# Transposes of K and Q by VectorE from 32x32 blocks loaded in place, instead of by TensorE, in a DeltaNet and feed-forward kernel

## The chip, the cores and the metric

The kernel runs on one core of one Trainium2 chip. The metric is the time on the device of one execution, in microseconds (us), as the median of several. The mean clock of TensorE over the whole span varied between 0.92 and 0.98 from run to run of the kernel before with no matching change of time; I read clocks only by stretch and never alone. In the views PE is TensorE's matmuls and PEld its weight loads; DVE is VectorE, ACT ScalarE, POOL GpSimd, SP SyncE, and a q after the name is the engine's DMA queue. The granted clock is the share of its full clock that TensorE was given (1.00 is all of it).

## The reference

Four batches, eight heads, 768 tokens, head size 48, all fp32. Attention is a delta rule, a recurrence over tokens; a layer norm and a two-layer feed-forward follow.

```python
for t in range(S):
    kt, vt, bt = k_n[:, :, t], v[:, :, t], beta[:, :, t, None]     # k_n: keys of length 1
    y[:, :, t] = einsum('bhd,bhde->bhe', q[:, :, t], state)
    v_old = einsum('bhde,bhd->bhe', state, kt)
    state = state + bt[..., None] * einsum('bhd,bhe->bhde', kt, vt - v_old)
# x = y with its heads side by side, (4, 768, 384); xn = layer norm of x times g_ln
out = x + maximum(xn @ w_ch1, 0) @ w_ch2                           # 384 -> 1536 -> 384
```

## The kernel before

The kernel works in 12 chunks of 64 tokens. Within a chunk the recurrence becomes a triangular system. `prep` forms K^T, Q^T and the products K·K^T (the "grams") and K·Q^T; `blocks` sends the grams through DRAM and inverts 32x32 blocks on VectorE in a long loop of short instructions; `join` combines the blocks by small matmuls (p_e, p_z); `recur` applies the state (p_by, p_u, p_s, p_by again); `ffn` is the feed-forward, the big matmuls p_h and p_o. The weights arrive as 64-bit floats and are converted on VectorE (w_sb). Everything is emitted by a plan with a time for each step, and the build lays out the order of instructions of each engine. Only the first part, up to the first joins, is held to the order of emission.

What the change touches:

```python
def load(dst, src, c, engs):                       # rows of 48 numbers into 64-wide slots
    for e in range(2):
        engs[e % len(engs)].dma_start(out=dst[e*C:(e+1)*C, :, 0:D], in_=src[...])
def load_all(c):                                   # 6 loads a chunk, all in SyncE's queue
    load(kpads[c % NKP], k, c, (nc.sync,)); load(qpads[c % NQP], q, c, (nc.sync,))
    load(vs[c], v, c, (nc.sync,))

def turned(c, g, n):                               # 4 TensorE transposes, 1 eviction by ScalarE
    p_t = ps_att([128, NP, 128], "p_t")
    for j in range(NP):
        nc.tensor.transpose(p_t[:, j], src[:, g*H+2*j : g*H+2*j+2], ident)
    nc.scalar.copy(made[c][0][g][:, :, n], p_t)

# in recur: 48 columns of keys a matmul, then two updates of the state
nc.tensor.matmul(p_s[DP*hp : DP*hp+D, ...], kp[half(e), 2*j+hp, 0:D], u[...])
for hp in range(2):
    nc.vector.tensor_tensor(out=new, in0=new, in1=p_s[DP*hp : DP*hp+D, ...], op=ALU.add)
# (cut)
first_join(0); first_join(1)                       # one after the other
```

## Time and profile before

| | before |
|---|---|
| median of 3 (range) | 675.39 us (674.75 to 676.48) |
| span of the profiled run | 673.2 us |
| start to the first weight converted after the joins | 86.2 us |
| from there to the end of the last conversion | 76.2 us |
| from there to the end ("late") | 510.8 us, TensorE busy 95% |

### The profile page before, as it was taken

The page shows a single profiled execution, that of the slowest core. Times are in us where ns is not written, and L with a number is a line of the kernel's source. Part 1 is how long each engine was busy: PE and PEld are TensorE (multiplying, and loading weights), DVE is VectorE, ACT ScalarE, POOL GpSimd, SP SyncE. Part 2 cuts the span into 40 slices and gives each one's busy share as a digit, 9 for nine tenths or more (in the row PEclk, how much of TensorE's full clock was granted, in tenths as well). Part 3 has the DMA queues.
Part 4 walks back from the last instruction along what each step waited for, and adds up shares of the span by engine and source line. Part 5 has one row for each costly group of instructions (what it writes and reads, how often), then busy time and mean ns, then how long its engine had stood idle before and what let it go on. Part 6 is the DMA issues. An engine that isn't in the chain of part 4 may idle for free.

```text
span 673.2 us, 18698 instructions
## 1 busy us (share of the span) xinstructions
PE 585.4 (87%) x8296; PEld 424.2 (63%) x8296; DVE 341.0 (51%) x870; ACT 180.5 (27%) x458; POOL 47.4 (7%) x78
## 2 busy tenths in 40 slices
PE   4214688968998989799899999899999899999997
PEld 4213576634865756686666786666876657768684
DVE  4542698999534695223964226944229742121100
ACT  3111343201332312241223432215421222213120
POOL 5000221111000101000100100101000000000000
PEclk9955577986999898599999999999999999999999
DMA  7975066851423415222305332023211020010000
GB/s 173 185 101 83 4 159 161 194 134 38 108 56 52 66 25 110 56 60 41 60 32 92 85 72 59 13 66 60 60 49 25 32 46 14 1 25 2 16 8 24
DMA packets 135824, 44.58 MB, mean 66 GB/s; under 512 B 128832, under 2 KB 131904, under 8 KB 135744
## 3 DMA queue, kind: packets, MB, share of 16 engines
q1 hardware_dynamic: 127392, 33.29, 25.5%
q0 software_dynamic: 1920, 9.44, 4.9%
q10 hardware_dynamic: 6432, 0.66, 0.8%
q8 instruction: 65, 1.06, 0.7%
q14 instruction: 15, 0.12, 0.1%
HBM read 29.48 MB, written 13.89 MB: 64 GB/s over the span
## 4 chain that ended last, share of the span: by engine, by line
PE 59%; DVE 26%; DMA 6%; issue 3%; SPq 3%; ACT 2%; DVEq 0%; ACTq 0%
PE p_o L631 20%; PE p_h L620 20%; DVE tmp L435 6%; DVE xb L440 6%; PE p_g L296 4%; PE p_t L285 3%; DMA kpad<-in_k_dram 2%; SPq L138 2%; PE p_e L465 2%; PE p_by L542 2%; PE p_z L506 2%; PE p_u L558 2%; DVE s L575 1%; PE p_s L569 1%; DVE full L259 1%
## 5 line engine op out<-in xcount | busy, mean ns | idle before, releaser
L631 PE MATMUL p_o<-w_sb,h_f 128*128 128x384 f32 x576 | 212.9, 507 | 9.2 <-DVE w_sb L263 9.2
L620 PE MATMUL p_h<-xnt,w_sb 128*128 128x256 f32 x864 | 210.5, 392 | 5.3 <-ACT h_f L625 5.1
L620 PEld LDWEIGHTS p_h<-xnt,w_sb 128*128 128x128 f32 x864 | 160.7, 193 | 32.5 <-ACT h_f L625 7.3
L631 PEld LDWEIGHTS p_o<-w_sb,h_f 128*128 128x128 f32 x576 | 104.2, 192 | 71.1 <-DVE w_sb L263 14.9
L625 ACT ACTIVATE h_f<-p_h 128x256 f32<-128x256 f32 x144 | 54.7, 383 | 129.1 <-PE p_h L620 128.7
L435 DVE TENSOR_TENSOR tmp<-xb,gb 128x31 f32<-128x31 f32 (+20 forms) x170 | 59.7, 351 | 4.2
L440 DVE TENSOR_TENSOR xb<-xb,tmp 128x31 f32<-128x31 f32 (+20 forms) x170 | 57.4, 338 | 4.4
L296 PE MATMUL p_g<-kqt 48*64 48x128 f32 (+1 forms) x896 | 33.3, 300 | 15.8 <-DVE pt L305 13.3
L296 PEld LDWEIGHTS p_g<-kqt 48*64 48x64 f32 x896 | 26.7, 163 | 24.0 <-DVE pt L305 12.6
L286 ACT COPY kqt<-p_t 128x512 f32<-128x512 f32 x48 | 27.9, 586 | 45.4 <-DVE w_sb L263 23.6
L638 DVE TENSOR_TENSOR o<-p_o,x_ln 128x384 f32<-128x384 f32 x24 | 13.3, 556 | 47.7 <-PE p_o L631 47.4
L575 DVE TENSOR_TENSOR s<-s,p_s 48x384 f32<-48x384 f32 x44 | 24.3, 552 | 25.9 <-PE p_s L569 25.3
L547 DVE TENSOR_TENSOR rhs<-v_raw,p_by 128x384 f32<-128x384 f32 x22 | 12.1, 552 | 45.6 <-PE p_by L542 45.6
L511 DVE COPY xt<-p_z 32x256 f32<-32x256 f32 x48 | 20.0, 416 | 27.7 <-PE p_z L506 27.1
L305 DVE TENSOR_TENSOR pt<-p_g,pmask 128x512 f32<-128x512 f32 x24 | 16.5, 688 | 34.1 <-ACT gsb L301 32.8
L525 DVE COPY u<-p_u 64x192 f32<-64x192 f32 x24 | 8.6, 359 | 47.7 <-ACT u L524 47.5
L542 PEld LDWEIGHTS p_by<-s,kqt 48*64 48x64 f32 x1408 | 23.2, 134 | 10.8 <-issue 8.9
L285 PE MATMUL p_t<-ident,qpad 128*128 128x128 f32 x96 | 17.7, 321 | 13.1 <-DMA qpad<-in_q_dram 12.5
L542 PE MATMUL p_by<-s,kqt 48*64 48x48 f32 x1408 | 26.4, 221 | 0.0
L465 PE MATMUL p_e<-xn,gsb 32*32 32x32 f32 x768 | 19.9, 207 | 7.3 <-DVE xn L457 7.0
L465 PEld LDWEIGHTS p_e<-xn,gsb 32*32 32x32 f32 x768 | 17.0, 121 | 13.2 <-issue 9.9
L285 PE MATMUL p_t<-ident,kpad 128*128 128x128 f32 x96 | 18.1, 323 | 7.8 <-POOL pmask L218 5.9
(78 smaller groups left out, 493.1 us busy)
## 6 DMA issues: line engine op xcount, KB each, us to landing
words<-in_moe_w_ch_dram POOLq DMA_DIRECT2D x24, 384.0 KB, 4.4
gd<-gsb SPq DMA_DIRECT2D x12, 512.0 KB, 3.5
qpad<-in_q_dram SPq DMA_DIRECT2D x24, 192.0 KB, 4.4
v_raw<-in_v_dram SPq DMA_DIRECT2D x24, 192.0 KB, 4.8
out_dram<-o SPq DMA_DIRECT2D x48, 96.0 KB, 2.2
kpad<-in_k_dram SPq DMA_DIRECT2D x22, 192.0 KB, 4.2
gb<-gd SPq DMA_DIRECT2D x40, 64.0 KB, 3.4
xd<-xb SPq DMA_DIRECT2D x5, 512.0 KB, 4.5
```

The costliest lines, as they stand in the source:

```text
L285: nc.tensor.transpose(p_t[:, j], src[:, h : h + 2], ident)
L286: nc.scalar.copy(made[c][0][g][:, :, n], p_t)
L296: nc.tensor.matmul(p_g[toks, hp, j, n0:n1], kqt[rows, j, 0, toks], kqt[rows, j, n0:n1, toks])
L435: nc.vector.tensor_tensor(out=t, in0=xb[:, :, 0:n, j : j + 1].to_broadcast([128, nb, n, w]), in1=gb[:, :, j : j + 1, j + 1 : L].to_broadca ...
L440: nc.vector.tensor_tensor(out=rest, in0=rest, in1=t, op=ALU.subtract)
L465: nc.tensor.matmul(p_e[r1, h % H], gsb[r0, h, BK:C], xn[r0, h])
L511: nc.vector.tensor_copy(out=xt[r0, g * H : (g + 1) * H, BK:C], in_=p_z[r0])
L542: nc.tensor.matmul(p_by[half(e ^ (hp & n)), hp, n, j], kqt[rows, j, n, half(e)], s[rows, e, j], start=(n == 0 and j == 0), stop=(n == 0), ...
L575: nc.vector.tensor_tensor(out=new, in0=new, in1=p_s[DP * hp : DP * hp + D, :, 0 : NP * D].rearrange("p e (j d) -> p e j d", d=D), op=ALU.add,)
L620: nc.tensor.matmul(p_h, w1_sb[:, t, f * 128 : (f + 1) * 128], xnt[:, t], start=(t == 0), stop=(t == KC - 1),)
L625: nc.scalar.activation(h_f, p_h, ACTF.Relu)
L631: nc.tensor.matmul(p_o, hs[f][:, g * 128 : (g + 1) * 128], w2_sb[:, f], start=(f == 0), stop=(f == FT - 1),)
```

## The change

The intent is to take 192 transposes and 48 evictions off TensorE and ScalarE. VectorE can transpose 32x32 blocks from SBUF to SBUF. If the DMA writes each 32-token by 32-feature block where its transpose belongs, 24 instructions do the whole. The keys as rows are still needed for norms and state; they are loaded later, unpadded, and p_s takes 64 columns of them, so that one update serves the whole state. The two first joins are interleaved, and the norms of the second chunk come after them. Not shown in the cut below: the first weight words are fetched later, and from chunk 2 on the raw loads, norms and scaling of a chunk are a step of their own (`prep_v`).

```diff
+def load_blocks(src, c, n, engs):                  # 8 DMAs for K, 8 for Q
+    dst = tblocks[(2 * c + n) % NTB]
+    for u in range(2):
+        for hp in range(2):
+            for m in range(2):
+                w = min(32, D - 32 * m)
+                engs[m % len(engs)].dma_start(out=dst[p0:p0+32, :, u, 0:w], in_=...)
+def load_turned(c):
+    load_blocks(k, c, 0, (nc.sync,))
+    load_blocks(q, c, 1, (nc.sync,))
-def turned(c, g, n):  # 4 x nc.tensor.transpose, nc.scalar.copy
+def turned(c, n):
+    nc.vector.transpose(made[c][0][:, :, n]..., tblocks[(2 * c + n) % NTB])
 ...
-    kp[half(e), 2 * j + hp, 0:D]
+    kp[half(e), h0 * D : h0 * D + DP]
-for hp in range(2):
-    nc.vector.tensor_tensor(out=new, in0=new, in1=p_s[...], op=ALU.add)
+nc.vector.tensor_tensor(out=s, in0=s, in1=p_s[...], op=ALU.add)
 ...
 next(inv)                     # first gathers
-for c in two: load(qpads[c], q, c, (nc.sync,))
+for c in two: load_blocks(q, c, 1, (nc.sync,))
+for c in two: load_kv(c)
 next(inv)
-(Q transposes by TensorE)
+for c in two: turned(c, 1)    # before the inverse loop, on its engine
 ...
+first joins 0 and 1 interleaved; after them:
+scale_v(1, norms(1), nc.vector)
 ...
-plan.once(times[0] - 20, load_all, chunks[0])
-plan.once(times[0] + 13 - 0.5, load_all, chunks[1])
+for i, c in enumerate(chunks):
+    plan.once(times[0] - 20 + 32.5 * i, load_turned, c)
```

More of the change, by code (lines that the diff above doesn't have):

```diff
@@ L108 @@
     const = ctx.enter_context(tc.tile_pool(name="const", bufs=1))
-    loads = ctx.enter_context(tc.tile_pool(name="loads", bufs=4))
+    loads = ctx.enter_context(tc.tile_pool(name="loads", bufs=3))
     work = ctx.enter_context(tc.tile_pool(name="work", bufs=2))
@@ L128, in ps_ffn @@
         return psum.tile(shape, FP32, name=name, tag="ffn", bufs=2)
-    NKP, NQP, NXT = 4, 2, 4
-    kpads = [const.tile([128, GH, DP], FP32, name=f"kpad{i}") for i in range(NKP)]
-    qpads = [const.tile([128, GH, DP], FP32, name=f"qpad{i}") for i in range(NQP)]
+    NXT, NTB = 4, 4
+    tblocks = [const.tile([128, GH, 2, 32], FP32, name=f"tb{i}") for i in range(NTB)]
+    NK = 3
+    kraws = [const.tile([128, GH * D + DP - D], FP32, name=f"k{i}") for i in range(NK)]
     vs = {}
-    def load(dst, src, c, engs):
+    def load_blocks(src, c, n, engs):
+        dst = tblocks[(2 * c + n) % NTB]
+        for u in range(2):
+            toks = slice(c * C + 32 * u, c * C + 32 * u + 32)
+            for hp in range(2):
+                for m in range(2):
+                    w = min(32, D - 32 * m)
+                    p0 = DP * hp + 32 * m
+                    engs[m % len(engs)].dma_start(
+                        out=dst[p0 : p0 + 32, :, u, 0:w],
+                        in_=src[:, hp::2, toks, 32 * m : 32 * m + w].rearrange("b j t d -> t (b j) d"),
+                    )
@@ L137, in load, with k_of, load_kv @@
+    def load(dst, src, c):
         for e in range(2):
-            engs[e % len(engs)].dma_start(
-                out=dst[e * C : (e + 1) * C, :, 0:D],
+            nc.sync.dma_start(
+                out=dst[e * C : (e + 1) * C],
                 in_=src[2 * e : 2 * e + 2, :, c * C : (c + 1) * C, :].rearrange("g h p d -> p (g h) d"),
             )
-    def load_all(c):
+    def k_of(c):
+        return kraws[c % NK][:, 0 : GH * D].rearrange("p (h d) -> p h d", d=D)
+    def load_kv(c):
+        load(k_of(c), k, c)
@@ L144, in load_all @@
         vs[c] = loads.tile([128, GH, D], FP32, name="v_raw")
-        load(kpads[c % NKP], k, c, (nc.sync,))
-        load(qpads[c % NQP], q, c, (nc.sync,))
-        load(vs[c], v, c, (nc.sync,))
-    for t in kpads[0:2]:
-        nc.vector.memset(t[:, :, D:DP], 0.0)
+        load(vs[c], v, c)
+    def load_turned(c):
+        load_blocks(k, c, 0, (nc.sync,))
+        load_blocks(q, c, 1, (nc.sync,))
+    for i in (0, 2, 1, 3):
+        for hp in range(2):
+            p0 = DP * hp + 32
+            (nc.vector if i in (0, 2) else nc.gpsimd).memset(tblocks[i][p0 : p0 + 32, :, :, D - 32 : 32], 0.0)
@@ L151 @@
     for c in range(2):
-        load(kpads[c], k, c, (nc.sync, nc.scalar))
-    for t in (*qpads, *kpads[2:]):
-        nc.gpsimd.memset(t[:, :, D:DP], 0.0)
+        load_blocks(k, c, 0, (nc.sync, nc.scalar))
     w1_sb = const.tile([128, KC, DFF], FP32, name="w1_sb")
@@ L174, in fetch_words @@
             )
-    for _ in range(3):
-        fetch_words()
     beta_b = const.tile([128, NSL, BK], FP32, name="beta_b")
@@ L223 @@
     xts = [const.tile([128, GH, C], FP32, name=f"xt{i}") for i in range(NXT)]
+    for t in kraws:
+        nc.gpsimd.memset(t[:, GH * D :], 0.0)
     for t in xts:
@@ L228 @@
         nc.gpsimd.memset(t, 0.0)
+    for _ in range(3):
+        fetch_words()
     scale_w = const.tile([128, KC + 1], FP32, name="scale_w")
@@ L276 @@
     made, grams, deep_pools = {}, {}, []
-    N_PREP = 1 + 2 * 3
-    def turned(c, g, n):
-        src = (kpads[c % NKP], qpads[c % NQP])[n]
-        p_t = ps_att([128, NP, 128], "p_t")
-        for j in range(NP):
-            h = g * H + 2 * j
-            nc.tensor.transpose(p_t[:, j], src[:, h : h + 2], ident)
-        nc.scalar.copy(made[c][0][g][:, :, n], p_t)
+    N_PREP = 4
+    def turned(c, n):
+        nc.vector.transpose(
+            made[c][0][:, :, n].rearrange("p i (u t) -> p i u t", t=32), tblocks[(2 * c + n) % NTB]
+        )
     def products(c, g, n0, n1):
-        kqt = made[c][0][g]
+        kqt = made[c][0]
         p_g = ps_two([128, 2, NP, 2, C], "p_g")
@@ L295, in products @@
                 toks = slice(C * e, C * e + C)
-                nc.tensor.matmul(
-                    p_g[toks, hp, j, n0:n1], kqt[rows, j, 0, toks], kqt[rows, j, n0:n1, toks]
-                )
+                i = (2 * e + g) * NP + j
+                nc.tensor.matmul(p_g[toks, hp, j, n0:n1], kqt[rows, i, 0], kqt[rows, i, n0:n1])
         heads = slice(g * H, (g + 1) * H)
@@ L311, in norms @@
     def norms(c):
-        kp = kpads[c % NKP]
         ksum = work.tile([128, GH], FP32, name="ksum")
@@ L316, in norms @@
             ksq = work.tile([128, H, D], FP32, name="ksq", bufs=1)
-            nc.scalar.square(ksq, kp[:, heads, 0:D])
+            nc.scalar.square(ksq, k_of(c)[:, heads])
             nc.vector.tensor_reduce(out=ksum[:, heads], in_=ksq, axis=mybir.AxisListType.X, op=ALU.add)
@@ L333, in new_chunk @@
         pool = deep_pools[0] if c % 4 == 0 and deep_pools else work
-        made[c] = ([pool.tile([128, NP, 2, 128], FP32, name="kqt", bufs=2 if pool is not work else 6) for _ in range(2)], [])
+        made[c] = (pool.tile([128, GH, 2, C], FP32, name="kqt", bufs=1 if pool is not work else 3), [])
     def prep(c):
         new_chunk(c)
-        scale_v(c, norms(c), nc.gpsimd)
-        yield
+        for n in range(2):
+            turned(c, n)
+            yield
         for g in range(2):
-            for n in range(2):
-                turned(c, g, n)
-                yield
             products(c, g, 0, 2)
@@ L346, in prep, with prep_v @@
         nc.sync.dma_start(out=grams[c][1], in_=grams[c][0])
+    def prep_v(c):
+        load_kv(c)
+        yield
+        with tc.issue_after(after) if c < 4 else nullcontext():
+            scale_v(c, norms(c), nc.gpsimd)
+        yield
     def prep_g(c):
         new_chunk(c)
-        for g in range(2):
-            turned(c, g, 0)
-            yield
+        turned(c, 0)
         for g in range(2):
@@ L492, in first_join @@
         nc.scalar.mul(es, p_e, -1.0)
+        yield
         p_z = ps_att([128, GH, FB], "p_z")
@@ L500, in first_join @@
             copy(out=xt[rows, :, c0 + FB : c0 + BK], in_=p_z[rows])
+        yield
     def last_z(xt, g, es, p_z, h):
@@ L528, in recur @@
     def recur(c, g):
-        kqt, pt = made[c][0][g], made[c][1][g]
+        kqt, pt = made[c][0], made[c][1][g]
         heads = slice(g * H, (g + 1) * H)
-        kp, xt, vv = kpads[c % NKP][:, heads], xts[c % NXT][:, heads], vs[c][:, heads]
+        kp, xt, vv = kraws[c % NK], xts[c % NXT][:, heads], vs[c][:, heads]
         s = states[g]
@@ L542, in recur @@
                         nc.tensor.matmul(
-                            p_by[half(e ^ (hp & n)), hp, n, j], kqt[rows, j, n, half(e)], s[rows, e, j],
+                            p_by[half(e ^ (hp & n)), hp, n, j], kqt[rows, (2 * e + g) * NP + j, n], s[rows, e, j],
                             start=(n == 0 and j == 0), stop=(n == 0), skip_group_check=True,
@@ L568, in recur @@
                 for hp, e in TILES:
+                    h0 = g * H + 2 * j + hp
                     nc.tensor.matmul(
-                        p_s[DP * hp : DP * hp + D, e, j * D : (j + 1) * D],
-                        kp[half(e), 2 * j + hp, 0:D], u[half(e), 2 * j + hp],
-                    )
-            for hp in range(2):
-                new = s[DP * hp : DP * hp + D]
-                nc.vector.tensor_tensor(
-                    out=new, in0=new,
-                    in1=p_s[DP * hp : DP * hp + D, :, 0 : NP * D].rearrange("p e (j d) -> p e j d", d=D),
-                    op=ALU.add,
-                )
+                        p_s[half(hp), e, j * D : (j + 1) * D],
+                        kp[half(e), h0 * D : h0 * D + DP], u[half(e), 2 * j + hp],
+                    )
+            nc.vector.tensor_tensor(
+                out=s, in0=s, in1=p_s[:, :, 0 : NP * D].rearrange("p e (j d) -> p e j d", d=D), op=ALU.add
+            )
             yield
@@ L653 @@
         for c in two:
-            first.spread(prep_g(c), 4, 4 * c, 4 * c + 4)
-        first.spread(weights(0, 3), 3, 0, 8)
+            first.spread(prep_g(c), 2, 4 * c, 4 * c + 4)
+        first.spread(weights(0, 3), 3, 8, 16)
         first.run()
@@ L659 @@
         for c in two:
-            load(qpads[c], q, c, (nc.sync,))
+            load_blocks(q, c, 1, (nc.sync,))
         for c in two:
-            vs[c] = loads.tile([128, GH, D], FP32, name="v_raw")
-            load(vs[c], v, c, (nc.sync,))
+            load_kv(c)
         next(inv)
         for c in two:
-            for g in two:
-                turned(c, g, 1)
+            turned(c, 1)
         for _ in inv:
@@ L670 @@
         for c in (2, 3):
-            load_all(c)
+            load_turned(c)
         load_beta()
-        knrms = []
-        for c in two:
-            knrms.append(norms(c))
-            for g in two:
-                products(c, g, 1, 2)
-        for c in two:
-            first_join(c)
+        for g in two:
+            products(0, g, 1, 2)
+        scale_v(0, norms(0), nc.vector)
+        joins = [first_join(c) for c in two]
+        next(joins[0])
+        for g in two:
+            products(1, g, 1, 2)
+        next(joins[0])
+        next(joins[1])
         joined = join(two)
         next(joined)
-        scale_v(0, knrms[0], nc.vector)
+        next(joins[1])
         next(joined)
-        scale_v(1, knrms[1], nc.vector)
-        for _ in joined:
-            pass
+        next(joined)
+        next(joined)
+        next(joined)
+        scale_v(1, norms(1), nc.vector)
     after = last[mybir.EngineType.DVE]
@@ L702 @@
         t0, t1 = starts[c], ends[c]
+        if c > 1:
+            plan.spread(prep_v(c), 2, t0 - 72, t0 - 12)
         plan.once(t0, begin, c)
```

## The prediction

> **What bounds the kernel now.** I first read parts 1 and 2 of the page, to see which engine is full and when:
>
> ```profile
> PE 585.4 (87%) x8296; PEld 424.2 (63%) x8296; DVE 341.0 (51%) x870; ACT 180.5 (27%) x458; POOL 47.4 (7%) x78
> ...
> PE   4214688968998989799899999899999899999997
> ...
> DVE  4542698999534695223964226944229742121100
> ...
> DMA  7975066851423415222305332023211020010000
> ```
>
> TensorE (PE) is full over the span but not everywhere: one slice is 16.8 us, and in the first five PE is mostly idle. VectorE (DVE) is full in slices 6 to 10. So I cut the span at the first matmul of the feed-forward stage (82 us) and at the last weight conversion (161.8 us), and asked for the busy time in the three stretches. Columns: stretch, length, then PE, PEld, DVE, ACT, POOL busy (instructions), granted clock, DMA share, GB/s.
>
> ```profile
> 0.00:82.00 82.00, 31.95 (x1148) 27.65 (x1148) 37.13 (x90) 19.13 (x43) 16.59 (x35) 0.72 0.65 112
> 82.00:162.40 80.40, 65.19 (x786) 44.84 (x782) 76.41 (x200) 20.55 (x51) 12.25 (x21) 0.80 0.57 139
> 162.40:674.00 511.60, 488.23 (x6368) 351.67 (x6368) 227.47 (x581) 140.87 (x364) 18.52 (x22) 0.98 0.22 47
> ```
>
> Three limits. **Start** (0 to 82): no engine is half busy; a chain of loads, DRAM round trips and short instructions sets the time. **Middle** (82 to 162): DVE is busy 76.4 of 80.4 us (95%), above all converting weights. **Late** (162 to the end): PE is busy 488 of 511.6 us (95%), so what PE is spared there comes off the end.
>
> The removed work, from the groups by line:
>
> ```profile
> L286 ACT COPY kqt<-p_t 128x512 f32<-128x512 f32 x48 | 27.9, 586 | 45.4 <-DVE w_sb L263 23.6
> L285 PE MATMUL p_t<-ident,qpad 128*128 128x128 f32 x96 | 17.7, 321 | 13.1 <-DMA qpad<-in_q_dram 12.5
> L285 PE MATMUL p_t<-ident,kpad 128*128 128x128 f32 x96 | 18.1, 323 | 7.8 <-POOL pmask L218 5.9
> L575 DVE TENSOR_TENSOR s<-s,p_s 48x384 f32<-48x384 f32 x44 | 24.3, 552 | 25.9 <-PE p_s L569 25.3
> ```
>
> These are 192 PE transposes, 35.8 us of PE busy time, with 48 evictions by ScalarE. The last line is the state update that the change merges from two instructions into one.
>
> ```profile
> L485 DVE STREAM_TRANSPOSE xn<-xt 128x1024 f32<-128x1024 f32 x2 | 2.5, 1240 | 0.0
> ```
>
> This is the price of the replacement: the kernel already has a 32x32-block transpose of 128x1024 on DVE, the shape of the new ones, at 1240 ns.
>
> **What the Trainium skill says.** "VectorE: DVE Perf Modes", section The three transpose paths: TensorE's full transpose goes to PSUM, VectorE's to SBUF but only in 32x32 blocks. The trace agrees: each four PE transposes have an eviction of 586 ns, and the DVE instruction writes SBUF itself. [...]192 B rows took 15 ns (median) but 19.7 on average[...]; 128 B packets (the DRAM round trips) took 13.5 and 64 B ones 10.3. "TensorE: Matmul & The Clock Gate", section LDWEIGHTS: the load time follows the number of columns. The trace agrees: 64-column groups (p_u) cost PE 13.93 us for 640, 48-column ones (p_s) 10.35 us for 576, or 21.8 and 18.0 ns each.
>
> **The change, part by part.**
>
> *Late stretch, PE.* The same windows for p_t alone give 7.37 us in the start, 7.91 in the middle and 19.94 in the late stretch (120 transposes, 30 groups of four). Busy spans overlap their neighbours; from one start to the next a group of four holds PE for 0.44 to 0.60 us (360.48 to 361.06, 387.92 to 388.36), say 0.55. So 30 x 0.55 = 16.5 us. Against it, p_s now loads 64 columns, not 48: 576 x (21.8 - 18.0) ns = +2.2 us. On DVE two transposes per chunk cost 2.5 us and the merged updates save 4 - 2 = 2 per chunk, 1.1 us; with DVE at 227 of 511 us that lies beside PE. One update fewer between p_s and the next p_by and no ACT copies in front of p_g may take 1.5 us from PE's small waits. Late: -16.5 + 2.2 - 1.5 = **-16 us**.
>
> *Middle, DVE.* PE loses 7.9 us there, but it waits for weights at the end (p_o for w_sb, 9.2 us in the waits), so that becomes idle time. DVE gains the transposes of chunks 2 and 3, 4 x 1.24 = 5.0, and loses four state updates, 2.2. The order of instructions shows weights and inverse steps interleaved nearly as before. I put this at **+2 us**.
>
> *Start.* Before, the chain runs: keys landed 11.6, transposes and products, both grams sent to DRAM at 17.3, blocks gathered 25.2, inverse loop 27.64 to 36.26, scattered back 42.7, norms and masked products, first-join transpose at 52.03 and 61.27, 32-wide joins from 70.5.
> (a) Keys: each row becomes 128 B + 64 B, about 25 ns for 19.7, so 4096 rows over 16 engines take 6.4 us for 5.0; but the weight words (1.15 MB, 2.9 us at 393 GB/s) are issued later and no longer mixed in. Transposing is 1.24 us for two PE groups and two copies. Grams about **-1 us**.
> (b) The order of instructions on DVE puts both Q transposes *before* the inverse loop, and the queue issues the 16 Q-block loads only after the gathers. The Q loads start near 22.5; at 0.55 us an issue (kpad issues took 0.60 and 0.65) that is 9 us, with 2 us to land: 33.3, plus 1.24, so the loop starts near 34.6 in place of 27.6. **+7 us.** Before, TensorE did the Q transposes beside the loop.
> (c) After the loop, masked products of chunk 0 fit under the round trip, only chunk 0's norms stand before the first join, and the second join overlaps the first. From the scattered inverse to the 32-wide join I count about 23 us (3.8 of norms and scaling, 1.24, 2.0 of p_e, some 3 of chunk 1's products, 2.4 of p_z, 1.7 of copies, 1.24, 0.7, gaps) where it was 27.8, and with (a) and (b) and small gaps recovered: **-10 us**; but the second norm, its scaling and two chunk-2 transposes move into the following joins, **+2.5 us**.
> Sum of the start: -1 + 7 - 10 + 2.5 = about **-2 us**, the least certain term.
>
> Total: -16 + 2 - 2 = -16, so 675.4 - 16 = **659 us**.
>
> **Rivals.** *The Q load stalls the inverse fully.* For it: DVE runs in strict order in this stretch, and the DMA is at 9 tenths or more when q and v were loaded before (20 to 34 us). If block loads are as slow per packet as whole rows (19.7 ns), 8192 packets take 10 us, and issue backpressure adds to it: the loop starts near 38, the start is 4 to 6 us worse than now, the total 666. *DVE becomes the bound further.* For it: 95% in the middle, and the inverse loops hold about 34 of 45 us of DVE in every other period. Against it: each inverse has 28 us of planned slack before its join. If each transpose of 1.24 us delays rhs or u by its length in DVE's queue on half of the 20 late occasions, 12 us are lost and the total is 671. *The queue of loads becomes a wait.* 20 load DMAs a chunk in place of six, 12 us of SyncE issue per 45 us; gathers and scatters share that queue. Before, SyncE mostly waited (142 us for finished outputs), so I expect it hidden; if not, 665 to 675. *The good case:* the Q blocks land by 30 us, PE's waits in the middle shrink too, and with clock dilation p_t is worth its full 19.9 + 7.9: 645.
>
> **Range and chances.** The late term is nearly sure in sign (10 to 19 us); start and middle together may be -10 to +10. That gives 642 to 674. 2% faster is below 661.9, just above my centre: 0.57. Within 2% is 0.39. Slower needs every rival at once: 0.04.
>
> **What would show it.** Right: PE busy near 552 (585 less 36, plus 2 to 3), ACT near 152, DVE near 359 (24 x 1.24 more, 12 less); late stretch near 496 us and still 95% PE; DVE idle before the first inverse loop, released by the Q-block DMA, for 5 to 8 us; new transposes at 1.24 us; p_s near 21.8 ns a matmul. Wrong: PE idle in the late stretch above 35 us, released by DVE or DMA; a middle longer by over 5 us; or a Q load that lands before the gathered blocks do. A different granted clock in the middle (0.80 now) would move the time with no cause in the change's own terms.

## More of the kernel before

The experiments lay on four chips, and the kernel before was run beside every set: its medians were 675.27, 675.04, 674.49, 675.63, 674.90 and 674.71 us (the second and third share seven runs), so chips are no concern here.

One more view matters for what came: how TensorE's instructions stand around a join. This is the timeline of PE (start, duration, line, output and inputs, number of matmuls):

```profile
363.61 0.69 PE L465 MATMUL p_e<-xn,gsb 32*32 32x32 f32 x32
364.24 0.91 PE L631 MATMUL p_o<-w_sb,h_f 128*128 128x384 f32 x2
365.08 0.69 PE L506 MATMUL p_z<-xt,es 32*32 32x32 f32 x32
365.70 0.91 PE L631 MATMUL p_o<-w_sb,h_f 128*128 128x384 f32 x2
366.54 1.10 PE L296 MATMUL p_g<-kqt 48*64 48x128 f32 x32
```

Between two dependent groups of small matmuls (p_z needs the eviction of p_e) stand two feed-forward matmuls, 0.91 us of work. The wait for the eviction is thereby filled, and no line has an idle time in brackets.

## The result, and the profile after

The changed kernel takes **725.35 us** (median of 4, 725.07 to 725.86) beside 675.27 us for the kernel before. The ratio is 1.074 (95% interval 1.0721 to 1.0758). No check of this run's result is on record; e1, e3 and e13, which differ from it only in the queue or the time of the loads, are correct. The prediction was 659 us, and 725 lies far outside its range.

The page of the kernel after:

```profile
span 724.1 us, 18501 instructions
PE 587.4 (81%) x8104; PEld 429.0 (59%) x8104; DVE 358.6 (50%) x874; ACT 152.8 (21%) x410; POOL 46.6 (6%) x81
...
PE   2004679837999987999887999887999867999997
...
PEclk9999999998999995899985899985899995999999
...
DMA packets 212240, 49.29 MB, mean 68 GB/s; under 512 B 205248, under 2 KB 208320, under 8 KB 212160
```

DVE is at 358.6 and ACT at 152.8, where 359 and 152 were predicted. PE has 192 instructions fewer and yet is busy as long as before (585.4). In the late part its row is no longer a row of nines: every six slices come two or three of six to eight, and in the same rhythm the clock has a 5 or an 8.

The busy time by stretch, for the kernel before and then for the kernel after. The stretches end at the first weight converted after the joins, at the end of the last conversion, and at the end of the span. The columns are those of the prediction's table.

```profile
0.00:86.20 86.20, 35.34 (x1248) 30.65 (x1248) 41.09 (x102) 20.68 (x48) 16.59 (x35) 0.71 0.64 110
86.20:162.40 76.20, 61.81 (x686) 41.84 (x683) 72.46 (x189) 19.00 (x46) 12.25 (x21) 0.82 0.59 143
162.40:673.20 510.80, 488.23 (x6368) 351.67 (x6368) 227.47 (x581) 140.87 (x364) 18.52 (x22) 0.98 0.23 47
```

```profile
0.00:95.70 95.70, 30.57 (x1231) 26.36 (x1235) 49.05 (x109) 15.02 (x37) 13.65 (x34) 1.00 0.58 102
95.70:170.80 75.10, 52.74 (x633) 34.90 (x625) 73.60 (x192) 13.21 (x35) 12.19 (x21) 0.98 0.62 144
170.80:724.10 553.30, 504.04 (x6248) 367.74 (x6248) 235.90 (x576) 124.59 (x338) 20.80 (x26) 0.91 0.27 52
```

Of the 50.9 us that the span grew, 9.5 arose before the conversions went on, 1.1 were regained during them, and 42.5 arose in the late stretch. There TensorE does exactly 120 matmuls fewer (6248 for 6368: the transposes) and is busy 16 us longer, at a mean granted clock of 0.91 for 0.98. Its idle time there is 49.3 us for 22.6.

Where in the late stretch? Four windows of 45 us, one chunk each by the plan, of which I show two:

```profile
315.00:360.00 45.00, 43.64 (x570) 30.54 (x562) 23.87 (x61) 11.02 (x31) 2.01 (x3) 1.00 0.33 60
360.00:405.00 45.00, 35.83 (x613) 27.58 (x613) 25.66 (x63) 9.68 (x26) 2.68 (x3) 0.70 0.47 90
```

The second holds the join: PE idle for 9 us, the granted clock 0.70. The Trainium skill ("TensorE: Matmul & The Clock Gate", section HAM oscillation) says that idle gaps of more than some 3.4 us bring TensorE's clock down to half. The trace agrees in the halving (the clock is 0.50 from 375.6 to 402.9 us) but not in the length of the gap: the clock falls after one of 2.72 us that ends at 375.20, before a p_g, and the gap of 3.65 us before a p_e comes only later. The same 2.72 us stand before the fall at 484.8 us. The longest gap of the late stretch is 8.9 us. The waits of each engine (waiting line, what released it, us in total, times, the longest):

```profile
PE p_g L318 <- DVE kqt L305: 34.1, 5, 20.6
PE p_e L487 <- DVE xn L479: 19.8, 4, 8.9
...
DVE rhs L571 <- PE p_by L566: 91.9, 10, 18.6
```

Of p_g's 34.1 us, 27.8 lie in the first 35 us of the span and only 6.3 in the late stretch; the other two lie wholly in the late stretch. There PE waits for DVE and DVE waits for PE, both far longer than before: DVE's wait at rhs was 45.6 us with 6.5 at most, PE's at p_e was 7.0 with 2.8 at most. Two engines that wait for each other, neither being full, point to the order of instructions. TensorE's timeline in the kernel after:

```profile
289.45 16.59 PE L641 MATMUL p_h<-xnt,w_sb 128*128 128x256 f32 x66
...
375.20 1.63 PE L318 MATMUL p_g<-kqt 48*64 48x128 f32 x32 [2.72 <-DVE kqt L305]
...
383.88 1.92 PE L487 MATMUL p_e<-xn,gsb 32*32 32x32 f32 x64 [3.65 <-DVE xn L479]
385.81 1.06 PE L530 MATMUL p_z<-xt,es 32*32 32x32 f32 x32
387.38 1.55 PE L582 MATMUL p_u<-rhs,xt 64*64 64x48 f32 x32 [0.51 <-DVE xt L535]
389.37 0.44 PE L605 MATMUL p_by<-u,pt 64*64 64x48 f32 x2 [0.43 <-ACT u L548]
```

Here the feed-forward matmuls stand in one block of 66, 16.6 us long. The next join, 94 us on, has none between its groups, where before there were two in each gap. VectorE, meanwhile, holds at rhs for p_by, which stands behind the block of 66. A query transpose, and after it the steps of the inverse, stand behind rhs. From 280 us on, the longest run of feed-forward matmuls with no other matmul between, away from the end, is 7.3 us (24 matmuls) before, and 17.0 us (66) after; such blocks of 16.5 to 17 us stand at 289, 398, 507 and 614 us, one for every two chunks. The first transposes of xn of two joins that lie four chunks apart stand at 355.7 and 542.8 us before, so 93.6 us for two chunks; after, at 383.1 and 598.8, so 107.9 us.

SyncE's queue in the same trace:

```profile
331.75 4.74 SPq L148 DMA_DIRECT2D tb<-in_k_dram  x8
336.53 5.02 SPq L148 DMA_DIRECT2D tb<-in_q_dram  x8
```

The 16 block loads of a chunk take 9.8 us of issue here, one after another, and stand in line with finished outputs and the gathers and scatters of the inverse. That was my first suspicion: late loads, or another order of instructions because of them.

The start, on DVE's timeline:

```profile
33.02 1.25 DVE L305 STREAM_TRANSPOSE kqt<-tb 128x1024 f32<-128x1024 f32 x1 [2.40 <-DMA tb<-in_q_dram]
37.32 1.25 DVE L305 STREAM_TRANSPOSE kqt<-tb 128x1024 f32<-128x1024 f32 x1 [3.06 <-DMA tb<-in_q_dram]
```

The inverse loop begins at 38.48 us (27.6 before, 34.6 predicted, 38 in a rival). The first xn transpose of the 32-wide joins comes at 70.2 (69.7 before). So the interleaved joins made good what the Q blocks cost, to within 0.5 us.

### The profile page after: what moved, and what is told of

Read it like the earlier page. It is cut to its first block, busy times and chain, and to the rows that moved or that the text cites. A ratio compares the mean times of both kernels' runs of the same rounds, so it can differ in the third digit from the quotient of the medians.

```text
span 724.1 us, 18501 instructions
## 1 busy us (share of the span) xinstructions
PE 587.4 (81%) x8104; PEld 429.0 (59%) x8104; DVE 358.6 (50%) x874; ACT 152.8 (21%) x410; POOL 46.6 (6%) x81
## 4 chain that ended last, share of the span: by engine, by line
PE 44%; DVE 30%; DMA 8%; issue 8%; SPq 7%; ACT 2%; ACTq 0%; DVEq 0%; POOL 0%; POOLq 0%
PE p_h L641 17%; PE p_o L652 15%; DVE tmp L457 8%; DVE xb L462 7%; SPq L148 5%; DVE kqt L305 2%; PE p_g L318 2%; PE p_z L530 2%; PE p_e L487 2%; PE p_u L582 2%; DMA tb<-in_q_dram 2%; PE p_by L566 2%; DMA xd<-xb 2%; DMA xt<-xd 1%; PE p_by L605 1%
## 5 line engine op out<-in xcount | busy, mean ns | idle before, releaser
L652 PE MATMUL p_o<-w_sb,h_f 128*128 128x384 f32 x576 | 207.5, 501 | 16.8 <-DVE w_sb L287 16.7
L641 PEld LDWEIGHTS p_h<-xnt,w_sb 128*128 128x128 f32 x864 | 168.3, 200 | 29.5 <-ACT xnt L629 2.1
L318 PE MATMUL p_g<-kqt 48*64 48x128 f32 (+1 forms) x896 | 35.8, 313 | 54.7 <-DVE kqt L305 34.1
L487 PE MATMUL p_e<-xn,gsb 32*32 32x32 f32 x768 | 23.5, 230 | 20.9 <-DVE xn L479 19.8
L325 DVE TENSOR_TENSOR pt<-p_g,pmask 128x512 f32<-128x512 f32 x24 | 16.6, 690 | 46.6 <-ACT gsb L321 39.6
L566 PEld LDWEIGHTS p_by<-s,kqt 48*64 48x64 f32 x1408 | 29.6, 151 | 15.6 <-issue 10.9
L305 DVE STREAM_TRANSPOSE kqt<-tb 128x1024 f32<-128x1024 f32 x24 | 29.8, 1241 | 13.8 <-DMA tb<-in_q_dram 9.4
L566 PE MATMUL p_by<-s,kqt 48*64 48x48 f32 x1408 | 34.9, 239 | 0.5 <-ACT x_ln L550 0.5
L487 PEld LDWEIGHTS p_e<-xn,gsb 32*32 32x32 f32 x768 | 20.8, 143 | 24.3 <-DVE xn L479 20.8
L321 ACT COPY gsb<-p_g 128x512 f32<-128x512 f32 x24 | 14.0, 584 | 73.7 <-PE p_g L318 73.6
L605 PEld LDWEIGHTS p_by<-u,pt 64*64 64x64 f32 x768 | 18.7, 155 | 13.0 <-issue 6.1
L605 PE MATMUL p_by<-u,pt 64*64 64x48 f32 x768 | 23.2, 243 | 3.2 <-ACT u L548 2.3
```

The costliest lines, as they stand in the source:

```text
L305: nc.vector.transpose(made[c][0][:, :, n].rearrange("p i (u t) -> p i u t", t=32), tblocks[(2 * c + n) % NTB])
L318: nc.tensor.matmul(p_g[toks, hp, j, n0:n1], kqt[rows, i, 0], kqt[rows, i, n0:n1])
L487: nc.tensor.matmul(p_e[r1, h % H], gsb[r0, h, BK:C], xn[r0, h])
L566: nc.tensor.matmul(p_by[half(e ^ (hp & n)), hp, n, j], kqt[rows, (2 * e + g) * NP + j, n], s[rows, e, j], start=(n == 0 and j == 0), stop= ...
L605: nc.tensor.matmul(p_by[half(e ^ hp), hp, 1, j], pt[half(e), 2 * j + hp], u[half(e), 2 * j + hp], start=(c == 0 and j == 0), stop=True, sk ...
L641: nc.tensor.matmul(p_h, w1_sb[:, t, f * 128 : (f + 1) * 128], xnt[:, t], start=(t == 0), stop=(t == KC - 1),)
```

## The experiments

The theory for the first set was: the order of TensorE's instructions, laid out anew because 32 small loads for two chunks stand in SyncE's queue, costs the late stretch. The rivals were that the loads land late, and that VectorE holds TensorE up by the transposes themselves. Unless said otherwise each kernel is the kernel after with the edit shown, and the result is correct. Ratios are to the kernel before.

**e1: the loads from chunk 4 on go out from GpSimd's queue.**

```diff
-load_blocks(k, c, 0, (nc.sync,))
+load_blocks(k, c, 0, (nc.gpsimd if c > 3 else nc.sync,))     # and q alike
```

> The changed kernel, but from chunk 4 on the block loads of keys and queries are issued from GpSimd's queue instead of SyncE's; nothing else is edited. Built, TensorE's instruction order is interleaved again: feed-forward runs of over 5 us fall from 7 (59 us of work) to 2 (25 us). Theory A (32 small loads per pair of chunks share SyncE's in-order queue with stores and the inverse's gathers, and this both delays the second chunk's transposes and bunches the order of instructions): 645 to 672 us, the late period back to 85 to 92 us per two chunks from 108.7. Theory B (VectorE's in-order queue with the new 1.24 us transposes is what delays the joins, whoever loads): above 705 us. Theory C (DMA traffic of the small packets): above 705 us, as the packets are the same.

Measured: 674.09 us, ratio 0.9992 (0.9963 to 1.002). One word took away 51 us. By stretch:

```profile
0.00:96.50 96.50, 30.55 (x1220) 26.03 (x1223) 49.44 (x110) 15.22 (x37) 27.25 (x54) 1.00 0.65 114
96.50:177.40 80.90, 56.99 (x647) 36.95 (x642) 79.82 (x201) 13.99 (x38) 33.82 (x51) 0.90 0.60 145
177.40:669.80 492.40, 469.91 (x6248) 336.59 (x6248) 229.30 (x566) 123.36 (x335) 70.59 (x104) 0.99 0.25 54
```

The late stretch is 492.4 us, 18 less than before, and two chunks take 90.7 us. The longest run of feed-forward matmuls from 280 us on is 8.0 us. But the conversions end at 177.4 instead of 162.4 us, so that nothing is left in sum. This settled that the transposes as such do not cost 50 us, but moved two things at once: the queue on the chip and the order from the build.

**e2 and e4: all engines held to the order of emission, the kernel after and, as a control, the kernel before.**

```diff
-plan.run()
+with in_this_order(tc):
+    plan.run()
```

> The changed kernel, loads still on SyncE's queue, but VectorE, ScalarE, TensorE and SyncE are held to the order in which the program text emits the instructions, also after the start. Theory A1 (the compiled order of TensorE's instructions is what costs the time: feed-forward matmuls bunched before the joins): 645 to 680 us. Theory A2 (SyncE's queue itself, on the chip, with loads behind stores that wait, is what costs it): above 700 us. Theory B (VectorE transposes): above 700 us.

> Control: the kernel before with the same forced order of instructions as in e2. If forcing the order is by itself neutral: 665 to 690 us. Then the difference to e2 is what the change is worth without the reordering: theory A1 has e2 faster than this by 10 to 25 us; B and A2 have e2 slower than this.

Measured: 804.03 us (1.1938, 1.1897 to 1.198) and 784.35 us (1.1632, 1.1588 to 1.1675). The order of emission is itself bad, by 109 us for the kernel before. So e2 says nothing on the change, and it was the control that showed it.

**e3: the block loads of the second chunk emitted 13 instead of 32.5 units after the first's.**

```diff
-plan.once(times[0] - 20 + 32.5 * i, load_turned, c)
+plan.once(times[0] - 20 + 13 * i, load_turned, c)
```

> The changed kernel with the block loads of the second chunk of a pair emitted 13 plan units after the first's instead of 32.5, still on SyncE's queue; the compiled order of TensorE stays bunched (6 feed-forward runs of over 5 us, 49 us). Theory A1 (bunched order): 700 to 725 us. Theory A2 (the second chunk's loads come too late): 655 to 690 us.

Measured: 724.02 us, 1.0741 (1.0703 to 1.0779), as after. The runs of feed-forward matmuls stay bunched (13.4 to 17.2 us). That the second chunk's loads are asked for late is not the cause.

**e5 and e6: order and queue apart.** After the plan's run I chained PE, DVE and ACT, but not SyncE, to an order recorded from another build. e5 has the loads in SyncE's queue with e1's order; e6 has them in GpSimd's queue with the order of the kernel after.

```diff
 plan.run()
+for engine, recorded in orders_of_the_other_build:
+    chain(instructions_of(engine), recorded)      # each after the one before it
```

> The changed kernel with every block load left on SyncE's queue, but TensorE, VectorE and ScalarE held, instruction by instruction, to the order that the compiler gave them in e1 (built: the orders of the three engines are the same as e1's, feed-forward runs of over 5 us 2). Theory A1 (the compiled order costs the time): 665 to 690 us, like e1's 674. Theory A2 (the loads in SyncE's queue cost it on the chip, whatever the order): above 700 us.

> The mirror of e5: block loads from chunk 4 on from GpSimd's queue as in e1, but the three engines held to the order of the changed kernel (built: the same 7 long feed-forward runs, 59 us). Theory A1 (order): 700 to 730 us. Theory A2 (queue): below 690 us.

Measured: e5 695.60 us, 1.0325 (1.0298 to 1.0351); e6 729.86 us, 1.084 (1.0798 to 1.0882). With the kernel after and e1:

| | loads in SyncE's queue | loads in GpSimd's queue |
|---|---|---|
| order of the kernel after | 725.4 | 729.9 |
| order of e1 | 695.6 | 674.1 |

With the bad order the queue gains nothing. With the good order and the old queue 30 us come back, and 21 more with the other queue. The late stretches of e5 and of e6 (columns as before):

```profile
194.17:693.20 499.03, 471.86 (x6248) 337.68 (x6248) 230.24 (x566) 123.29 (x335) 19.89 (x24) 0.98 0.27 53
172.94:728.00 555.06, 505.35 (x6248) 368.85 (x6248) 236.82 (x575) 124.02 (x338) 82.52 (x122) 0.90 0.23 49
```

The late stretch follows the order: 499.0 us in e5 against 553.3 in the kernel after, with the same queue, and 555.1 in e6 against 492.4 in e1. So the order is the cause there, within some 7 us. The queue's own 21 us show only under the good order, and most of them before the late stretch: in e5 the last conversion ends at 194.2 us against 177.4 in e1. Nearly all of these 16.8 us are one wait of VectorE, for eight key loads that left SyncE's queue late:

```profile
140.28 4.59 SPq L148 DMA_DIRECT2D tb<-in_k_dram  x8
146.62 1.25 DVE L305 STREAM_TRANSPOSE kqt<-tb 128x1024 f32<-128x1024 f32 x1 [15.75 <-DMA tb<-in_k_dram]
```

In e1 the same transpose starts at 131.2 us.

**e13 and e14: another queue, and half of the loads.** e13 is e1 with ScalarE's queue in place of GpSimd's; in e14 only the key blocks go there and the query blocks stay with SyncE.

```diff
-load_blocks(k, c, 0, (nc.sync,))
+load_blocks(k, c, 0, (nc.scalar if c > 3 else nc.sync,))     # e13: q alike; e14: q unchanged
```

> The kernel after with one edit: the block loads of chunks from 4 on are issued by ScalarE's queue, not SyncE's (the first run of this kind used GpSimd's and gave 674). Theory (the order of TensorE's instructions, set by how many loads stand in SyncE's queue): any other queue brings the interleaved order back, so the late stretch falls to about 91 us per two chunks, and as ScalarE does not slow VectorE's conversions as GpSimd's issues seemed to, they end near 168 and not 177: 669 to 674. Rival (GpSimd's queue is special, or the gain was chance): 690 or more.

> As e13, but only the 16 key blocks of two chunks go to ScalarE's queue and the 16 query blocks stay in SyncE's: half the small loads. Its build shows an interleaved order. Theory (order): near e13, at most 6 us above it for the loads that still queue behind finished outputs: 670 to 680. Rival (each small load in SyncE's queue costs its own time on the chip, in proportion to their number): half way between 725 and e13, about 697.

Measured: e13 673.49 us, 0.9984 (0.9958 to 1.001); e14 670.45 us, 0.9945 (0.9931 to 0.996). GpSimd was not special. Half of the small loads may stay in SyncE's queue and the whole loss is gone: it does not go with their number but comes with the order, which is interleaved in both (longest runs from 280 us on 9.4 and 8.1 us). e13's conversions ended at 173.4, not near 168 as expected, and its late stretch took 501.3.

**e7, e8 and e9: the early part.** In e1 the conversions end 15 us later than before. e7 is e1 with the Q transposes after the first inverse loop, and the raw keys and values of chunk 1 loaded after it. e8 is e7 and takes the second chunk's norms out from in front of the conversions. e9 is e8 with ScalarE's queue.

```diff
 next(inv)
-for c in two: turned(c, 1)
 for _ in inv: pass
+for c in two: turned(c, 1)                # e7
+load_kv(1)                                # e7
 ...
-    scale_v(1, norms(1), nc.vector)
 after = last[mybir.EngineType.DVE]        # the conversions wait for this instruction
+    scale_v(1, norms(1), nc.vector)       # e8
```

> e1 with the start mended: the two Q transposes on VectorE stand after the first inverse loop, and chunk 1's raw keys and values are loaded after the loop too. In e1 as in the changed kernel the loop starts at 38.5 us, where the kernel before had 27.6, because VectorE waits for the Q blocks. Theory (the stall is on the path that sets the end): loop starts near 31 us, time 664 to 669 us, 5 to 10 below e1's 674. Rival (the start is hidden behind the weight conversions of the middle, which have their own length): within 2 us of e1.

> e7, and the weight conversions no longer queue behind chunk 1's norms and scaling, which leave the held order. In the kernel before the conversions resumed at 83 us and ended at 162; in e1 at 92.6 and 177. Theory (the end of the conversions is the end of the middle stretch, and from there on TensorE is full): conversions resume by 80 us and end by 163, time 650 to 662 us. Rival (the middle is bound by the chain of joins and recurrences): not below e7 by more than 2 us.

> e8 with the block loads of chunks 4 and later on ScalarE's queue instead of GpSimd's. In e8 GpSimd issues them for some 0.6 us each in the middle stretch, and VectorE's weight conversions there took 4.1 us a piece where the kernel before had 3.8. Theory (GpSimd's work beside VectorE slows VectorE): conversions back to 3.8 us a piece, 660 to 668 us. Rival (the conversions are slowed by VectorE's own additional transposes and inverse steps): 669 to 674 us, like e8's 671.

Measured: e7 674.82 us, 1.0014 (0.9988 to 1.004); e8 671.34, 0.9967 (0.9937 to 0.9996); e9 667.74, 0.9877 (0.9833 to 0.9922). In e7 the loop starts at 31.1 us, 7.4 earlier than in e1, and the total does not move. The conversions do come earlier (from 90.2 us for 96.5, to 171.6 for 177.4), but the late stretch is 500.7 us for 492.4. So an earlier end of the conversions is not by itself a gain; why the late stretch grew I did not isolate. In e8 they go on 5.3 us earlier than in e7 (84.9 for 90.2), where 80 was expected. In e9 the last ends at 161.5 us (167.1 in e8), a conversion takes 3.8 us for 4.1, as expected, and the late stretch is 500.0. That GpSimd's issues slow the conversions is not shown: the same change of queue from e1 to e13 took them only from 4.02 to 3.96 us.

**e10, e12: parts of the change alone, with TensorE's transposes.** e10 is the kernel before with the 64-column p_s and the single update of the state. e12 has the interleaved first joins as well, with the conversions not behind the second norms.

```diff
-kp[half(e), 2*j+hp, 0:D]
+kp[half(e), 2*j+hp, 0:DP]
-for hp in range(2): nc.vector.tensor_tensor(out=new, in0=new, in1=p_s[half of the rows], op=ALU.add)
+nc.vector.tensor_tensor(out=s, in0=s, in1=p_s[...], op=ALU.add)
```

> The kernel before with one part of the change alone: one state update over 128 partitions instead of two over 48, and p_s with 64 columns of weights. My prediction gave it -1.1 us of VectorE per chunk, beside the path, +2.2 us of TensorE in all, and up to -1.5 of waits: 673 to 677 us. If the shorter path from p_s to the next p_by counts in full, 22 x 0.55 us: 660 to 666 us.

> The kernel before with the interleaved first joins and the merged state update, TensorE transposes and loads as before; the weight conversions do not queue behind the second chunk's norms. The joins are worth 5 to 10 us of the start by my prediction; if the start counts: 664 to 670 us. If not (the middle has its own length): 672 to 677 us.

Measured: e10 675.25 us, 1.0004 (0.9966 to 1.0042), with VectorE at 329.0 us (12 less); e12 673.31 us, 0.9959 (0.9913 to 1.0004). The state update is neutral. e9 seemed to beat e12 by its transposes. But e9 has another queue too, which e15 takes up.

**e11: a hybrid, wrong.** Chunks 0 to 3 by TensorE as before, VectorE's transposes from chunk 4 on.

```diff
+if c >= 4: turned_v(c, n)      # by VectorE, blocks in ScalarE's queue
+else:      turned(c, g, n)     # by TensorE
```

> A mix: start and chunks 0 to 3 as in the kernel before (TensorE transposes), the merged state update, and from chunk 4 on the block loads on ScalarE's queue with VectorE transposes, values loaded later. Built, TensorE's order is interleaved (2 long feed-forward runs). Theory (the change is worth what TensorE is spared in the late stretch, as long as the order stays interleaved and the middle is not lengthened): conversions end near 162, late stretch 495 to 503 us, time 655 to 666 us. Rival (what TensorE is spared comes back as waits): 670 us or more.

Measured: 666.34 us, but the result is wrong (relative error 0.488), so this time decides nothing. I later found the fault: with three block buffers, the query load of one chunk overwrote a key buffer that was still to be transposed.

**e15 and e16: the missing control, and the best version again.** e15 is e12 with its key, query and value loads of chunks from 4 on in ScalarE's queue; e16 is e9 unchanged. Both have the same joins, the same state update and loads in ScalarE's queue; they differ in who transposes (and in what is loaded for it: e16's raw keys and values stay in SyncE's queue, and its norms and scaling are in the separate step).

```diff
-load(kpads[c % NKP], k, c, (nc.sync,))
+load(kpads[c % NKP], k, c, (nc.scalar if c > 3 else nc.sync,))    # e15; q and v alike
```

> The control that was missing: the best version (transposes by VectorE, loads by ScalarE's queue, 668) differs from e12 (PE transposes, 673) in two things. Here e12 with its key, query and value loads of chunks from 4 on issued by ScalarE's queue. If the transposes themselves are worth the late 11 to 14 us, this stays at 672 to 675. Rival (it is the queue alone that gains): 664 to 668, and then VectorE's transposes are worth nothing.

> The best correct version (e9) again, unchanged, with more rounds on the same chip as e13 and e15: 667 to 669, ratio to before 0.985 to 0.992 with an interval clear of 1. Rival: e9's interval was chance, and the ratio is 0.995 or above.

Measured on one chip: e15 **668.21 us**, 0.9904 (0.9871 to 0.9938); e16 **666.79 us**, 0.9884 (0.9869 to 0.9899). The rival that I had thought unlikely holds to within 1.4 us, which these intervals do not tell from nothing. The two by stretch, e15 first:

```profile
0.00:82.90 82.90, 35.09 (x1186) 30.04 (x1186) 40.41 (x100) 20.19 (x46) 16.42 (x35) 1.00 0.65 111
82.90:155.70 72.80, 58.48 (x742) 41.87 (x742) 70.06 (x182) 19.32 (x48) 11.94 (x21) 0.95 0.63 153
155.70:666.20 510.50, 487.91 (x6368) 350.53 (x6368) 220.61 (x570) 141.09 (x364) 17.28 (x22) 0.98 0.22 47
```

```profile
0.00:85.40 85.40, 26.97 (x1154) 23.49 (x1154) 46.71 (x104) 13.71 (x33) 13.67 (x34) 1.00 0.64 111
85.40:163.60 78.20, 55.72 (x702) 38.41 (x702) 73.37 (x188) 15.18 (x40) 11.79 (x21) 1.00 0.82 169
163.60:665.20 501.60, 473.55 (x6248) 338.77 (x6248) 238.34 (x586) 123.99 (x337) 22.44 (x26) 0.98 0.27 53
```

With VectorE's transposes the late stretch is 8.9 us shorter (TensorE busy 14.4 us less), but it begins 7.9 us later: 2.5 us up to the first conversion and 5.4 in the conversions, where VectorE is busy 94 to 96% of the time. What is gained late is given back earlier, where the work was moved to. From e1 to e7 the two traded against each other as well, so they need not be two separate effects.

**e17 and e18.** e17 is the hybrid with its fault mended (the second chunk's loads emitted after the first chunk's transposes) and the start of e15. e18 is the kernel before with the change of queue alone.

```diff
-plan.once(times[0] - 20 + 13 * i, load_turned, c)
+plan.once(times[0] - 20 + 23.5 * i, load_turned, c)     # e17
```

> The hybrid again, with its fault mended (a query load had overwritten a key buffer that was still to be transposed): chunks 0 to 3 by PE as before, from chunk 4 on VectorE's transposes with loads in ScalarE's queue, start and state update as in e12 and e15. From e15 against e16: VectorE's transposes cost the start and the conversions 7.9 us and save 8.9 us after them. If those two are separate, the hybrid has the early part of e15 (155.7 us to the last conversion) and the late part of e16 (501.6): 657 to 661. Rival (what is spared late was only work put off, so that the end depends on the total alone, or the last conversions come later for the loads): 665 to 669.

> The kernel before with one edit: key, query and value loads of chunks from 4 on issued by ScalarE's queue. e15 had this and the joins and the state update as well (668). If the queue alone makes that gain: 667 to 671. If it needs the interleaved joins, whose conversions start earlier: 673 to 676.

Measured: e17 667.34 us, 0.9888 (0.9867 to 0.9909), correct; e18 675.59 us, 1.0005 (0.9978 to 1.0033). The hybrid has the short late stretch (497.6 us), but not the early end of e15: its last conversion ends at 166.5 us. So I missed again by some 8 us: the early cost does not come off by leaving the first four chunks as they were. What in e17 delays the conversions I did not isolate. e18 says that the queue alone gains nothing with large loads; whether e15's gain over e12 (668.2 against 673.3, on two chips, intervals overlapping) is the queue together with the joins or chance stays open.

## Why the prediction was wrong

The stretches of all kernels with a correct result, but for e2 and e4, in us. All but the last row have the interleaved order. "End" is the end of the last conversion.

| transposes by | kernels | end | late |
|---|---|---|---|
| TensorE | before, e10, e12, e15, e18 | 162.4, 163.1, 159.4, 155.7, 162.5 | 510.8, 512.1, 513.8, 510.5, 514.1: mean 512.3 |
| VectorE | e1, e13, e14, e5 (start of the kernel after) | 177.4, 173.4, 170.9, 194.2 | 492.4, 501.3, 496.2, 499.0 |
| VectorE | e7 to e9, e16, e17 (start mended) | 171.6, 167.1, 161.5, 163.6, 166.5 | 500.7, 502.5, 500.0, 501.6, 497.6: mean of all nine 499.0 |
| VectorE | after, e3, e6 (bunched order) | 170.8, 170.8, 172.9 | 553.3, 554.7, 555.1 |

**The step that failed first: the order of TensorE's instructions.** The prediction took the late stretch as the old order less some instructions. It compared the order only for VectorE, in the start and in the middle ("weights and inverse steps interleaved nearly as before"). The rival that named the right place, "The queue of loads becomes a wait", was dismissed ("I expect it hidden; if not, 665 to 675"). It was thought of as a delay on the chip. The runs show a different thing: with the 32 small loads in SyncE's queue the build lays out feed-forward matmuls in blocks of 17 us, and the joins bare. Late stretch 553.3 against 501.3 in e13, which differs in the queue of those loads alone: 52 us. That the order carries it is shown by e5 and e6 (499.0 and 555.1), that each of three reliefs of the queue restored it by e1, e13 and e14. The delay on the chip that the rival named exists (15.75 us in e5), but under the order of the kernel after, moving the loads gained nothing (e6). A sign of being wrong that the prediction had named appeared: TensorE was idle in the late stretch for 49.3 us, above its 35, 19.8 of them at p_e for VectorE. Its busy time was 587.4 us, not 552. Why the build chooses that order was only argued: presumably its own estimate of the time makes the loads, and what depends on them, late. No run here shows it.

**The late term, -16: mechanism right, size somewhat smaller.** With the good order, nine kernels average 499.0 us against 512.3, so some -13. In the cleanest pair it is -8.9. TensorE's busy time fell by 14.4 us there, near the 16.5 predicted for the transposes, but 5.5 of it came back as idle time.

**The middle, +2, and the start, -2: their sum was mis-sized.** With the start of the kernel after, the conversions end at 170.8 to 177.4 us in place of 162.4 (e5 with its wait apart): 8 to 15 us, where 0 was predicted. The term that was too small is the "+2.5" for the second norms, scaling and chunk 2's transposes ahead of the conversions. The first weight after the joins is converted at 93.5 to 96.5 us for 86.2, so 7 to 10. e8 shows 5.3 of them to be the second norms and scaling. In the mended pair (e15, e16) the conversions' own 5.0 for the transposes fits (the stretch is 5.4 longer, with VectorE busy 3.3 more).

**Right parts.** The transposes took 1241 ns (1240 predicted). VectorE and ScalarE came within 1 us of their sums. The state update is neutral (e10), as its +2.2 and -1.5 on TensorE's path nearly sum to. The Q blocks stall the inverse loop, by 11 us where 7 were said, and the interleaved joins make it good. Their issue and landing were right (8.4 and 2.2 us for 9 and 2), but they went out at 27.1 us, not 22.5, behind gathers that were themselves later than before (18.8 to 27.1 us for 17.7 to 23.7): "grams about -1" was wrong. The rival's 38 was met by luck, for its slow packets did not come: the blocks' packets took 10.8 and 13.2 ns on average, not 19.7.

**Readings.** The prediction's first cut, 82 us, is not the first matmul of the feed-forward stage: the first p_n stands at 88.2 us and the first p_h at 95.7. Nothing rests on it. 192 B rows took 19.7 ns on average before and 16.6 after, with the same median of 15.

**Together.** Order about +52, late gain -9.5 (e13 against before), early cost +8.4: the span grew by 50.9 (the three add up by the way they are cut). With the order mended and nothing else, -9.5 and +11 leave e13 level with the kernel before. The best version, e16, is 1.2% faster than the kernel before and 8% faster than the kernel after. e15 has 1.0% without VectorE's transposes.

## What to carry to other kernels

When a change alters how many transfers stand in a queue, compare the built order of every engine before predicting, the bounding one first, and look for long unbroken blocks of the filler work. Moving work from the bounding engine to another is worth only what the other can bear in the stretch where it is itself the bound. An experiment that moves two things needs the control that moves one of them: here it turned "the transposes gain 1%" into "they gain nothing that can be told from noise".

## What the Trainium skill lacked or had wrong

- "DMA: Bandwidth & Descriptors", section Issuing engines are not separate DMA queues, says that issuing from several engines saves only the issuing time of the sequencer. The issue took 9.8 us a chunk here, yet moving it to another engine was worth 52 us (725.35 to 673.49 us), mainly through the order that the build then laid out (e5, e6). With the order held, loads that stood long in the queue still cost VectorE one wait of 15.75 us (e5). With six large loads a chunk the same move was worth nothing (675.59 us, e18). No page that I read says that the choice of queue can change the order of compute instructions.
- "VectorE: DVE Perf Modes", section The three transpose paths, gives a 128x128 bf16 case. For fp32 the runs show 1241 ns for 128x1024 on VectorE. On TensorE four 128x128 fp32 transposes held the engine 0.44 to 0.60 us, with 586 ns of eviction beside it.
- No page that I read compares the price of issuing small loads by engine: 487 ns on SyncE, 318 to 405 on ScalarE (e9, e13, e16), 651 on GpSimd (e1; all medians of the block loads). The eight early ones on ScalarE took 510 in the kernel after.
- "TensorE: Matmul & The Clock Gate", section HAM oscillation: its figure of some 3.4 us for a harmful gap was too long here. The clock fell to half at 375.6 us after a gap of 2.72 us.
